# Zero-tile products in TensorE's early gaps and two moved weight steps, in a delta-rule attention kernel followed by two feed-forward layers

## The chip, the cores and the metric

The kernel runs on one core of a Trainium2 chip. The metric is the device time of one execution in microseconds (us), the median of several runs.

## What is computed

A delta-rule attention over 4 batches, 8 heads, 768 steps and head size 48; its output, 3072 tokens of 384 numbers, goes through a feed-forward layer of width 2048 and then through four experts of width 1024, mixed per token. All inputs are float32 but the first layer's two weight matrices, which arrive as float64.

```python
for t in range(S):                       # attention, per batch and head
    kt, vt, bt = (k_n[:, :, t], v[:, :, t], beta[:, :, t, None])
    y[:, :, t] = np.einsum('bhd,bhde->bhe', q[:, :, t], state)
    v_old = np.einsum('bhde,bhd->bhe', state, kt)
    state = state + bt[:, :, :, None] * np.einsum('bhd,bhe->bhde', kt, vt - v_old)
h = x @ w_in                             # first layer
x = (h * (1.0 / (1.0 + np.exp(-1.702 * h)))) @ w_out
for e in range(E):                       # four experts
    out += p[:, e:e + 1] * (np.maximum(x @ w1[e], 0.0) @ w2[e])
```

## The kernel before, in words

**Attention.** The 768 steps are cut into 12 units of 64 (u = 0 to 11), each worked for all 32 heads at once. Within a unit the steps depend on each other through a triangular matrix, which is inverted. Units come in pairs (w = 0, 2, 4, ...), and two units make a tile of 512 tokens. For the first pair `queue_first_inverse` runs the inverse on DVE: fourteen steps (L724, L726), `end` (L731), `to_rows` (L685, a transpose), `turn` (L750, another, once per unit). Then TensorE (PE) joins the halves of each matrix in `first` (L769) and `second` (L778), with a copy between them (`out1`, ACT) and a multiply-add behind them (`out2`, L783, DVE). `queue_q` multiplies keys with queries (L491, PE) and masks the products on DVE (L496, four times 0.7 us a unit).

`queue_chain` does the rest of a unit in two halves hu = 0 and 1: `solve` (L881, PE), copies of its result (`solved`, L184), `cross` (L896, PE), a subtraction (`rest`, L874, DVE), `solve` again and its copies, `fourth` (a copy into `stage`, L184), `read` (L912 and L913, PE), which makes the output rows, and `write` (L936, PE), which updates the state. For u = 0 and 1 the output rows go straight into the first layer's input: `take_x` (L184, `xs<-y`, three copies a half, a high part) and `take_rest` (L930, DVE, the low part). `direct[0]` is the list of these twelve tasks of unit 0.

**First layer.** Its width is cut into 16 blocks f = 0 to 15 of 128. A tile takes `layer1` (L1089, `ph`), the activation (`gate`: L1211, L1213, L1214) and `layer2_1` (L1196, `px`) for each block. Numbers are split in a high and a low part, and three products of the parts stand for one (`PASSES`). The first two tiles' first eight blocks go in halves of 256 tokens, so that unit 0 alone lets the layer begin. From there PE does the layer's products with the remaining attention woven in, and then the experts (L1323, L1353).

**Weights.** A block's weights come as float64 and are decoded on the chip in `queue_w1`: `load` (a DMA of 768 KB), `small` (ACT, L293) on the upper words and `low` (ACT, L296) on the lower ones, `shift` (DVE, L300) which joins them, `hi` (ACT, L305) and `lo` (DVE, L308), the two parts. `low` waits for the load and for the inverse's beginning, not for `small`. Blocks 0 and 15 land in the tile `raw`, the others in six buffers `rw`. Blocks 2 to 6 have a `touch` (L274, a DVE memset of one column) ahead of the load, which waits for one of five `marks`, in this order: the inverse's `begin`, its seventh step, the first `turn`, the last `first` of unit 0, the `out2` of unit 0. Block 7 and those after it wait for the `lo` of six blocks earlier.

**What sets the order.** Each engine runs its instructions in the order in which they were issued, and so does SP, which starts the DMAs. A planner (`Order`, `Task`) fixes that order when the program is made: each task has an engine or a choice of two, a cost, tasks that it waits for and a priority (small goes first). The planner keeps a clock per engine; whenever one is free it issues the task with the smallest priority among those ready at that time. Unit 0's chain has priority 0, `take_x` and `take_rest` have -2, the weights 6 (blocks 0 and 1), 16 (2 to 7) and 33. Until the first layer begins, PE tasks count double (`slow`).

Of the kernel before, what the change touches and what calls it, by code (L numbers as in the profile page):

```python
# [7 lines left out]
F32 = mybir.dt.float32  # L8
# [19 lines left out]
class Order:  # L28
# [14 lines left out]
    def task(self, fn, eng, cost, deps=(), lat=0.15, prio=0, slack=0.5, can=None, extra=0.4):  # L43
        t = Task(self, fn, eng, cost, [d for d in deps if d is not None], lat, prio, slack, can, extra)
        return t
# [106 lines left out]
def delta_attention_moe_moe_kernel(  # L152
# [12 lines left out]
    nc = tc.nc  # L165
# [92 lines left out]
    def queue_w1(f, after):  # L258
# [56 lines left out]
        if wide:  # L315
            a = task(small, "ACT", 0.83, (dep,), **kw)
            b = task(low, "ACT", 0.9, (dep, begun[0]), **kw)
            dep = task(shift, "DVE", 0.88, (a, b), **kw)
# [50 lines left out]

    NR, zeros = {}, {}  # L370
    spare = wp.tile([128, 1536], F32, name="sp", tag=f"w{RAW - 1}")
    jmask = spare[:, 0:SB * SB // 4].rearrange("p (a b) -> p a b", a=SB // 2)
# [96 lines left out]
    def queue_q(u):  # L469
# [11 lines left out]
        for o in range(2):  # L481
# [19 lines left out]
            if len(visits) == whole:  # L501
                t = task(lambda fs=tuple(visits): weave(fs), "PE", 0.9 if u < 2 else 1.3,
                         (*placed[u], lq, begun[0], *(ends[-1:] if u > 1 else ())), prio=p + 1,
                         can=lambda: None if u > 1 and not od.moe else some_free(banks(), whole))
                for c, f in masks:
                    c.setdefault("end", []).append(task(f, "DVE", 0.69, (t, zeros["pm"]), prio=p + 1))
                    ends.append(c["end"][-1])
                visits.clear()
                masks.clear()
# [177 lines left out]
    def queue_first_inverse(us):  # L687
# [65 lines left out]

        marks.append(turned[0])
        merged, products = [], []
        turns[w] = turned[0]
        for c, u in enumerate(us):
# [4 lines left out]
            def first(gn, c=c, ends=ends):  # L762

                if not gn.start:
                    cell["p", c] = bank([128, 2, NP, H], ends)
                t = cell["p", c]
                for g in range(NP)[gn]:
                    for r in range(0, 128, SB):
                        mm(t[r:r + SB, 0, g, :], lhsT=GG[w][r:r + SB, c * NP + g, :],  # L769
                           rhs=cell["d"][r:r + SB, c * NP + g, 0:H], start=True, stop=True, tile_position=(r, r))  # L770

            def out1(e, gs=gs, c=c):
                copy(e, cell["d"][:, gs, 0:H], cell["p", c][:, 0])

            def second(gn, c=c, u=u):
                for g in range(NP)[gn]:
                    for r in range(0, 128, SB):
                        mm(cell["p", c][r:r + SB, 1, g, :], lhsT=cell["d"][r:r + SB, c * NP + g, :],  # L778
                           rhs=Tb[u][r:r + SB, g, H:], start=True, stop=True, tile_position=(r, r))

            def out2(u=u, c=c):
# [29 lines left out]
    def queue_chain(u):  # L811
# [153 lines left out]
        for hs in [halves[0:1], halves[1:2]] if u < 2 else [halves]:  # L965
            n = len(hs)

            def both(name, *args, hs=hs):
                return lambda: weave([lambda h=h: h[name](*args) for h in hs])

# [20 lines left out]
            else:  # L991
                bs = [lv]
            a = task(both("solve", 0), "PE", 0.4 * n, (*bs, invdone[u]), prio=p, can=None if u else room)
            bs = solved_tasks(a, not u)
            a = task(both("cross"), "PE", 0.38 * n, (*bs, *crossed[u]), prio=p)
            bs = [task(h["rest"], "DVE", 0.47, (a,), prio=p) for h in hs]
            a = task(both("solve", 1), "PE", 0.4 * n, bs, prio=p)
            for h in hs:
# [95 lines left out]
    with tc.manual_schedule():  # L1094
# [32 lines left out]
        for n, fn, cost in (("j", set_j, 0.6), ("q0", lambda: E_.memset(PQ[0], 0.0), 1.85),  # L1127
                            ("su", lambda: E_.memset(SU, 0.0), 1.4), ("st", lambda: E_.memset(stage, 0.0), 1.4),
                            ("pm", set_p, 2.1), ("q1", lambda: E_.memset(PQ[1], 0.0), 1.85), ("h", set_h, 1.0),
                            ("g", set_g, 1.1)):  # L1130
            zeros[n] = task(fn, "POOL", cost, (), prio=2)
        od.clk["POOL"], od.clk["HW"] = 0.8, 1.1

# [333 lines left out]
```

## Time and profile before

| | |
|---|---|
| median of 3 runs | 1365.65 us (1365.31 to 1365.78) |
| profiled execution, its own time | 1365.22 us |
| its span, first to last instruction | 1363.3 us |
| PE busy | 1332.3 us, 98% |
| DVE, ACT, POOL busy | 612.2, 423.1, 221.3 us |
| DMA | 63.30 MB |

The profile has a row for each group of instructions: the line of the program that made it, the engine, the tiles written and read (`out<-in`, buffer numbers left out), how many, and the time. PE is the matrix product, PEld the loading of its weights, SPq the queue that issues DMAs. In a timeline each row is a run of equal instructions: start, length, what it is, and in brackets how long the engine had been idle before it and what ended that. A float32 product stands as two matmul records, a product of the split parts (fp32r) as one.

### The profile page before, as it was taken

The page shows a single profiled execution, that of the slowest core. Times are in us where ns is not written, and L with a number is a line of the kernel's source. Part 1 is how long each engine was busy: PE and PEld are TensorE (multiplying, and loading weights), DVE is VectorE, ACT ScalarE, POOL GpSimd, SP SyncE. Part 2 cuts the span into 40 slices and gives each one's busy share as a digit, 9 for nine tenths or more (in the row PEclk, how much of TensorE's full clock was granted, in tenths as well). Part 3 has the DMA queues.
Part 4 walks back from the last instruction along what each step waited for, and adds up shares of the span by engine and source line. Part 5 has one row for each costly group of instructions (what it writes and reads, how often), then busy time and mean ns, then how long its engine had stood idle before and what let it go on. Part 6 is the DMA issues. An engine that isn't in the chain of part 4 may idle for free.

```text
span 1363.3 us, 28151 instructions
## 1 busy us (share of the span) xinstructions
PE 1332.3 (98%) x12376; PEld 1118.1 (82%) x12376; DVE 612.2 (45%) x1049; ACT 423.1 (31%) x790; POOL 221.3 (16%) x408
## 2 busy tenths in 40 slices
PE   5899999999999999999999999999999999999998
PEld 4788898778787888788888888888888888888888
DVE  7888584663735224223333234433343333233443
ACT  6873442432424334312222122222222221112111
POOL 4295748055181000000000000000000000000000
PEclk9999999999999999999999999999999999999999
DMA  7640412220201013000010000010010000011111
GB/s 238 217 132 14 113 29 76 63 64 2 74 17 40 5 76 124 8 9 31 31 42 20 1 20 31 32 38 14 0 31 31 32 20 8 0 31 31 32 31 47
DMA packets 36411, 63.30 MB, mean 46 GB/s; under 512 B 18688, under 2 KB 20160, under 8 KB 36288
## 3 DMA queue, kind: packets, MB, share of 16 engines
q1 hardware_dynamic: 36288, 61.50, 14.9%
q8 instruction: 97, 1.59, 0.5%
q14 instruction: 26, 0.21, 0.1%
HBM read 52.58 MB, written 7.91 MB: 44 GB/s over the span
## 4 chain that ended last, share of the span: by engine, by line
PE 92%; DVE 4%; DMA 1%; ACT 1%; issue 1%; SPq 0%; DVEq 0%; ACTq 0%
PE ph L1089 43%; PE po L1323 24%; PE px L1196 14%; PE po L1353 5%; PE y L913 2%; PE ch L881 1%; PE ch L867 1%; PE gp L491 1%; PE ch L896 1%; PE ch L936 1%; DMA rw<-in_w_dram 1%; DVE scr L581 1%; PE gp L554 1%; DVE scr L685 0%; DVE scr L184 0%
## 5 line engine op out<-in xcount | busy, mean ns | idle before, releaser
L1089 PE MATMUL ph<-xs,w 128*128 128x512 f32 (+1 forms) x2736 | 651.3, 380 | 1.7 <-ACT x L184 0.8
L1089 PEld LDWEIGHTS ph<-xs,w 128*128 128x128 f32 x2736 | 494.2, 188 | 96.8 <-ACT x L184 1.2
L1384 DVE SCALAR_TENSOR_TENSOR hh<-ph,hh 128x512 fp32r<-128x512 f32 x192 | 132.5, 690 | 503.4 <-ACT hh L1383 503.4
L1323 PE MATMUL po<-hh,w 128*128 128x512 f32 x1440 | 352.4, 389 | 0.0
L1323 PEld LDWEIGHTS po<-hh,w 128*128 128x128 f32 x1440 | 270.4, 188 | 56.0
L1383 ACT ACTIVATE hh<-ph 128x512 fp32r<-128x512 f32 x192 | 114.8, 598 | 616.7 <-PE ph L1089 616.7
L1196 PE MATMUL px<-gh,w 128*128 128x512 f32 (+1 forms) x1008 | 228.7, 364 | 1.0 <-DVE gh L1214 0.8
L1196 PEld LDWEIGHTS px<-gh,w 128*128 128x128 f32 x1008 | 170.7, 188 | 31.6 <-DVE gh L1214 2.1
L1214 DVE TENSOR_TENSOR gh<-ph,gh 128x512 fp32r<-128x512 f32 (+1 forms) x112 | 68.7, 613 | 149.2 <-ACT gh L1213 148.0
L1211 ACT ACTIVATE ph<-ph 128x512 f32<-128x512 f32 (+1 forms) x112 | 58.4, 521 | 176.0 <-PE ph L1089 164.7
L660 POOL TENSOR_TENSOR scr<-scr,itmp 128x30 f32<-128x30 f32 (+9 forms) x150 | 83.9, 559 | 11.8
L658 POOL TENSOR_TENSOR itmp<-scr 128x30 f32<-128x30 f32 (+9 forms) x150 | 79.5, 530 | 11.2
L1353 PE MATMUL po<-w,hh 128*128 128x384 f32 x384 | 73.9, 342 | 0.0
L1353 PEld LDWEIGHTS po<-w,hh 128*128 128x128 f32 x384 | 69.3, 188 | 2.4
L1213 ACT CAST gh<-ph 128x512 fp32r<-128x512 f32 (+1 forms) x112 | 58.8, 525 | 3.5
L184 ACT COPY su<-ch 64x384 f32<-64x384 f32 (+2 forms) x59 | 27.2, 462 | 63.2 <-PE ch L881 62.5
L1183 DVE TENSOR_TENSOR xs<-x,xs 128x512 fp32r<-128x512 f32 x72 | 45.3, 684 | 0.0
L1182 ACT CAST xs<-x 128x512 fp32r<-128x512 f32 x72 | 39.7, 619 | 0.0
L496 DVE TENSOR_TENSOR pq<-gp,pmask 64x512 f32<-64x512 f32 x48 | 33.1, 689 | 7.0 <-PE gp L491 6.1
L250 DVE TENSOR_TENSOR w<-raw,w 128x768 fp32r<-128x768 f32 x32 | 30.7, 958 | 10.2 <-ACT w L249 9.4
L184 DVE COPY su<-ch 64x384 f32<-64x384 f32 (+2 forms) x45 | 24.2, 537 | 21.3 <-PE ch L881 20.4
L953 DVE TENSOR_TENSOR su<-su,ch 48x384 f32<-48x384 f32 x44 | 24.3, 552 | 20.5 <-PE ch L936 10.3
(133 smaller groups left out, 740.8 us busy)
## 6 DMA issues: line engine op xcount, KB each, us to landing
raw<-in_we_dram SPq DMA_DIRECT2D x32, 384.0 KB, 2.9
rw<-in_w_dram SPq DMA_DIRECT2D x14, 768.0 KB, 4.6
raw<-prd SPq DMA_DIRECT2D x20, 256.0 KB, 3.1
k<-in_k_dram SPq DMA_DIRECT2D x12, 384.0 KB, 4.8
kt<-in_kt_dram SPq DMA_DIRECT2D x24, 192.0 KB, 5.0
pq<-in_q_dram SPq DMA_DIRECT2D x24, 192.0 KB, 3.5
v<-in_v_dram SPq DMA_DIRECT2D x12, 384.0 KB, 3.2
out_dram<-oacc SPq DMA_DIRECT2D x80, 48.0 KB, 1.7
```

Source lines behind the costliest of these rows:

```text
L184: (nc.scalar.copy if e == "ACT" else nc.vector.tensor_copy)(out=out_, in_=in_)
L658: E.tensor_tensor(out=tv, in0=x[:, j:j + 1, j + 1:].broadcast_to([128, m, r]), in1=x[:, 0:m, j:j + 1].broadcast_to([128, m, r]), op=ALU.mult)
L660: E.tensor_tensor(out=x[:, 0:m, j + 1:], in0=x[:, 0:m, j + 1:], in1=tv, op=ALU.add)
L1089: mm(ps, lhsT=w[:, a, kk * 128:(kk + 1) * 128], rhs=xs[kk][:, b, cs], start=kk == 0 and i == 0, stop=kk == KD - 1 and i == 2)
L1196: mm(px[d][:, cs], lhsT=w[:, a, 384 + d * 128:384 + (d + 1) * 128], rhs=gh[:, b, 0:cs.stop - cs.start], start=f == 0 and i == 0 and cs.sta ...
L1211: a = task(lambda: nc.scalar.activation(out=ph, in_=ph, func=AF.Gelu_apprx_sigmoid), "ACT", 0.05 + 0.43 * c, (pe,), **kw)
L1213: a = task(lambda: nc.scalar.copy(out=hi, in_=ph), "ACT", 0.05 + 0.43 * c, (a,), **kw)
L1214: a = task(lambda: nc.vector.tensor_tensor(out=lo, in0=ph, in1=hi.bitcast(F32), op=ALU.subtract), "DVE", 0.07 + 0.53 * c, (a,), **kw)
L1323: mm(po[kk], lhsT=w[:, a, 384 + kk * 128:384 + (kk + 1) * 128], rhs=hh[:, c, :], start=f == 0 and i == 0, stop=f == F2 - 1 and i == 2)
L1353: mm(ps, lhsT=hh[:, a, b * 128:(b + 1) * 128], rhs=w[:, c, 384:768].rearrange("p (k a i) -> p a k i", a=4, k=KD), start=f == 0 and i == 0, ...
L1383: nc.scalar.activation(out=hh[:, 0, :], in_=ph, func=AF.Relu)
L1384: nc.vector.scalar_tensor_tensor(out=hh[:, 1, :], in0=ph, scalar=0.0, in1=hh[:, 0, :].bitcast(F32), op0=ALU.max, op1=ALU.subtract)
```

## The change

Three things are changed.

- A tile `still` of zeros (one of the two `gh` buffers, set by one DVE memset at the very start) and a PSUM tile `idle` (one of the two `ph` buffers). `fill(n)` multiplies the zeros with themselves n times, 128 x 128 by 512 columns, into `idle`, which nobody reads. The planner is not told of it. It stands behind unit 1's key-query products (8), behind unit 0's `first` and `second` (2 each), and in unit 0's second half behind `solve`, `cross` and `solve` (2 each): 18 products.
- `small` of blocks 7 and later waits, in the planner, for `direct[0]` too.
- The third mark is the inverse's `end` in place of the first `turn`: block 4's `touch` and load wait for that.

```diff
         if wide:
-            a = task(small, "ACT", 0.83, (dep,), **kw)
+            a = task(small, "ACT", 0.83, (dep, *(direct[0] if f >= 7 else ())), **kw)
             b = task(low, "ACT", 0.9, (dep, begun[0]), **kw)
             dep = task(shift, "DVE", 0.88, (a, b), **kw)
...
     NR, zeros = {}, {}
+    still = ghp.tile([128, 2, TT], F32R, name="gh", tag="gh")[:, 0]
+    idle = psh.tile([128, TT], F32, name="ph", tag="ph")
+
+    def fill(n):
+        for _ in range(n):
+            mm(idle, lhsT=still[:, 0:128], rhs=still, start=True, stop=True)
+
...
             if len(visits) == whole:
-                t = task(lambda fs=tuple(visits): weave(fs), "PE", 0.9 if u < 2 else 1.3,
+                def products(fs=tuple(visits)):
+                    weave(fs)
+                    if u == 1:
+                        fill(8)
+
+                t = task(products, "PE", 0.9 if u < 2 else 1.3,
...
-        marks.append(turned[0])
+        marks.append(ended[w])
         merged, products = [], []
...
+                if not c:
+                    fill(2)
 
             def out1(e, gs=gs, c=c):
...
+                if not c:
+                    fill(2)
 
             def out2(u=u, c=c):
...
-            def both(name, *args, hs=hs):
-                return lambda: weave([lambda h=h: h[name](*args) for h in hs])
+            def both(name, *args, hs=hs, more=0):
+                def products():
+                    weave([lambda h=h: h[name](*args) for h in hs])
+                    if not u:
+                        fill(more)
+
+                return products
...
-            a = task(both("solve", 0), "PE", 0.4 * n, (*bs, invdone[u]), prio=p, can=None if u else room)
+            a = task(both("solve", 0, more=2 if hs[0]["hu"] else 0), "PE", 0.4 * n, (*bs, invdone[u]), prio=p, can=None if u else room)
             bs = solved_tasks(a, not u)
-            a = task(both("cross"), "PE", 0.38 * n, (*bs, *crossed[u]), prio=p)
+            a = task(both("cross", more=2 if hs[0]["hu"] else 0), "PE", 0.38 * n, (*bs, *crossed[u]), prio=p)
             bs = [task(h["rest"], "DVE", 0.47, (a,), prio=p) for h in hs]
-            a = task(both("solve", 1), "PE", 0.4 * n, bs, prio=p)
+            a = task(both("solve", 1, more=2 if hs[0]["hu"] else 0), "PE", 0.4 * n, bs, prio=p)
...
+        nc.vector.memset(still.bitcast(F32), 0.0)
         od.clk["POOL"], od.clk["HW"] = 0.8, 1.1
```

## Rows read from the trace of the kernel before

**Rows 1.** The page, part 1: busy us, share of the span, instructions.

```profile
PE 1332.3 (98%) x12376; PEld 1118.1 (82%) x12376; DVE 612.2 (45%) x1049; ACT 423.1 (31%) x790; POOL 221.3 (16%) x408
```

**Rows 2.** Busy time by stretch: length; PE, PEld, DVE, ACT, POOL; granted clock, DMA.

```profile
53.30:1363.30 1310.00, 1301.92 (x11231) 1090.81 (x11231) 567.92 (x948) 386.42 (x719) 204.43 (x370) 1.00 0.13 39
```

**Rows 3.** Timeline of PE, 24 to 54 us: start, length, what, idle before.

```profile
24.91 2.27 PE L491 MATMUL gp<-pq,kt 48*64 48x64 f32 x61 [2.80 <-issue]
29.92 1.90 PE L769 MATMUL gp<-scr,scr 32*32 32x16 f32 x128 [2.74 <-DVE rw L274]
32.30 1.14 PE L778 MATMUL gp<-scr,scr 32*32 32x16 f32 x67 [0.48 <-ACT scr L184]
35.54 1.04 PE L778 MATMUL gp<-scr,scr 32*32 32x16 f32 x61 [2.10 <-issue]
37.30 1.50 PE L881 MATMUL ch<-v,scr 32*32 32x48 f32 x64 [0.72 <-issue]
39.59 1.75 PE L896 MATMUL ch<-su,g 32*32 32x48 f32 x64 [0.80 <-ACT su L184]
...
45.05 0.49 PE L912 MATMUL y<-pq,stage 128*64 128x64 f32 x4 [1.04 <-DVE stage L184]
...
50.37 1.64 PE L936 MATMUL ch<-su,k 64*48 64x48 f32 x64
52.62 0.38 PE L1089 MATMUL ph<-xs,w 128*128 128x256 f32 x1 [0.61 <-ACT xs L184]
53.30 0.86 PE L1089 MATMUL ph<-xs,w 128*128 128x256 f32 x5 [0.29 <-DVE xs L930]
```

**Rows 4.** Groups by line, 45 to 50.3 us, then 78.6 to 86 us.

```profile
L912 PE MATMUL y<-pq,stage 128*64 128x64 f32 x48 | 5.2, 317 | 1.0 <-DVE stage L184 1.0
...
L912 PE MATMUL y<-pq,stage 128*64 128x64 f32 x48 | 3.0, 227 | 0.3 <-DVE xs L930 0.3
```

**Rows 5.** Busy time, 45 to 50 us: the column behind POOL's is the granted clock.

```profile
45.00:50.00 5.00, 4.95 (x92) 4.95 (x94) 4.43 (x5) 4.43 (x10) 0.87 (x1) 1.00 0.83 282
```

**Rows 6.** The page, part 5: count | busy us, mean ns of one | idle.

```profile
L1089 PE MATMUL ph<-xs,w 128*128 128x512 f32 (+1 forms) x2736 | 651.3, 380 | 1.7 <-ACT x L184 0.8
```

**Rows 7.** Timeline of DVE, 24 to 100 us.

```profile
26.17 0.69 DVE L731 TENSOR_TENSOR scr<-scr,bt 128x512 f32<-128x512 f32 x1
...
32.66 2.79 DVE L496 TENSOR_TENSOR pq<-gp,pmask 64x512 f32<-64x512 f32 x4
36.71 0.48 DVE L783 SCALAR_TENSOR_TENSOR scr<-gp,hmask,scr 128x256 f32<-128x256 f32 x1 [1.25 <-PE gp L778]
...
46.16 0.96 DVE L308 TENSOR_TENSOR w<-rw,w 128x768 fp32r<-128x768 f32 x1 [0.30 <-ACT w L305]
...
52.97 0.67 DVE L930 TENSOR_TENSOR xs<-y,xs 128x128 fp32r<-128x128 f32 x3
```

**Rows 8.** The page, part 3: queue, kind: packets, MB, share of 16 engines.

```profile
q8 instruction: 97, 1.59, 0.5%
```

**Rows 9.** The DMA queues between 33.2 and 33.5 us.

```profile
q1 hardware_dynamic: 9, 0.04, 34.6%
q8 instruction: 1, 0.02, 19.4%
```

**Rows 10.** Timeline of SP's DMA issues, 0 to 60 us; rows merge several issues.

```profile
29.82 7.75 SPq L222 DMA_DIRECT2D rw<-in_w_dram  x3
...
47.15 6.26 SPq L222 DMA_DIRECT2D rw<-in_w_dram  x3
```

**Rows 11.** Timeline of ACT, 0 to 60 us.

```profile
34.32 0.89 ACT L293 ACTIVATE rw<-rw 128x768 f32<-128x768 f32 x1 [2.08 <-DMA rw<-in_w_dram]
...
37.07 0.94 ACT L293 ACTIVATE rw<-rw 128x768 f32<-128x768 f32 x1 [1.09 <-DMA rw<-in_w_dram]
38.27 1.27 ACT L184 COPY su<-ch 32x192 f32<-32x192 f32 x4 [0.25 <-PE ch L881]
...
51.49 0.93 ACT L293 ACTIVATE rw<-rw 128x768 f32<-128x768 f32 x1 [0.69 <-DMA rw<-in_w_dram]
52.30 0.61 ACT L184 CAST xs<-y 128x128 fp32r<-128x128 f32 x3
```

## The prediction

> **What bounds the kernel now.** I read the page's busy times first: PE is busy 98% of the span, no other engine half of it [rows 1]. The busy time by stretch then says where PE's idle time is: from 53.30 us to the end PE is idle for 1310.00 - 1301.92 = 8.1 us in all [rows 2]. Before 53.30, where the first layer's second product starts [rows 3], it waits most of the time. So the time is the moment at which PE's unbroken work begins, plus about 1310 us of products that this change leaves alone. A microsecond saved ahead of 53.30 is a microsecond off the total, provided that DVE, ACT and the weights are as much earlier as PE.
>
> PE's timeline shows what comes before [rows 3]: the halves of the inverse are joined (L769, L778), with a stop of 2.10 us in the middle that no semaphore explains; then unit 0's chain, the reads from 45.05, the writes from 50.37, and the first layer at 52.62, which waits for ACT's rows and then for DVE's.
>
> **The clock.** The granted clock reads 1.00 from the start, at 45 to 50 us too [rows 5], but the products disagree. The 48 records of L912, with as many of L913 between them, take 5.2 us for unit 0 and 3.0 us for unit 1 [rows 4]: PE is at the lower of its two levels (1.2 GHz) in the first case and at the upper (2.4 GHz) in the second. I go by the durations. That is the slack the 18 zero products can take: they would have PE at the upper level some 20 us earlier.
>
> **Zero products, the first eight.** They start when unit 1's products end, 24.91 + 2.27 = 27.18 [rows 3], ahead of `first`, which can start at 29.92. L1089 has 651.3 us for 2736 products, most of them 512 columns wide: 0.24 us at the upper level [rows 6], so 0.48 at the lower, an estimate. Eight end between 29.1 and 31.0. `first` starts up to 1.1 us late; I take 0.6 (the level rising on the way). Once it has risen, `first` is at most half of its 1.90 us shorter, 0.95 [rows 3]. The two roughly cancel: 0, bounds -0.9 and +1.1. The memset of the tile is one DVE instruction at the start, hidden behind DVE's wait for the first load; without that cover it would cost as much as another 128 x 512 DVE instruction, 0.69 us [rows 7].
>
> **The ten others** stand behind `first` and `second` and in the second half's steps, two at a time, 0.5 us at the upper level and 1.0 at the lower, where PE waits 0.48, 0.72 and 0.80 us anyway [rows 3]. Upper: 0. Lower: 0.2 to 0.5 each, five times at most, of which the ACT steps below hide most: 0 to 2.0. I take 0.
>
> **The earlier load of block 4.** `end` is over at 26.17 + 0.69 = 26.86 [rows 7]; the load is issued near 27 and no longer at 29.82 [rows 10], 2.9 us sooner. On SP it now goes ahead of a load of unit 2's keys, which nobody needs for 20 us. ACT's first step on it, 34.32 after 2.08 us of waiting [rows 11], moves ahead of `out1` in ACT's order, near 31.4: `out1` may be up to 1 us later, hidden by what follows. What I expect it to move is the stop of 2.10 us in `second`. The queue q8 carries 97 packets of 1.59 MB / 97 = 16.4 KB [rows 8], and PE has 12376 matmuls and as many weight loads [rows 1]: 24752 / 97 = 255 instructions a packet. It is PE's program, in blocks, and the packet of that moment goes between 33.2 and 33.5 us [rows 9], when block 4's packets are just through. With that load out of the way the stop shrinks; I take 0.8 us left, bounds 0 and 2.10. The next to be late is DVE: its eight masks end at 32.66 + 2.79 = 35.45, so `out2` gains 36.71 - 35.45 = 1.26 us at most [rows 7], 0 at least. I take 1.2.
>
> The Trainium skill, in "Runtime: NRT & Kernel Launch", section "Instruction fetch mechanics", says that the program is fetched in blocks of 16 KiB ahead of need, "mostly hidden". The packet size agrees; the 2.10 us do not. By that rule the stop is something else and this part gains nothing.
>
> **What becomes of the 1.2 us.** ACT's copies of the first `solve` (38.27) stand behind block 5's `small`, which waits for its load until 37.07 [rows 11]; that load is issued between DVE's two sets of masks, whose time does not change. So the copies start at about 37.9, 0.4 sooner. The 1.2 come back only in part: block 6's load follows `out2`, so ACT is through with that block about 0.9 us sooner. Against it stand three shifts in the planner's order, which I followed with its costs alone (an order, no time): the second half's `rest` goes ahead of block 0's `lo`, block 5's `shift` ahead of block 1's `lo`, and `fourth` moves from DVE to ACT, behind the copies of both halves. Reads begin between 44.0 and 45.4, where they began at 45.05 [rows 3]; I take 44.8.
>
> **The reads** gain 5.2 - 3.0 = 2.2 us if the upper level holds until then [rows 4], 0 if not. They end near 48 and not at 50.3.
>
> **The rows and block 7.** ACT, in order, has `small` of block 7 at 51.49, after 0.69 us of waiting for the load, and the second half's rows behind it at 52.30 [rows 11]. The change makes `small` wait for the rows; `low`, its twin, still waits for the load alone. By the planner's costs block 7's load is issued at 45.50 (2.0 and 1.5 us: `low` ready at 49.00), ACT is free at 49.12 and the rows are ready at 49.45: `low` takes the place that `small` leaves, of about the same length. So the rows still stand behind that load, which follows block 1's `lo` (46.16 + 0.96 = 47.12 [rows 7]; issued at 47.15 [rows 10]) and lands 51.49 - 47.15 = 4.34 us after its issue. With block 1's `lo` ending between 46.3 and 47.7, `low` begins at 50.6 to 52.0, the rows 0.81 later (52.30 - 51.49), and DVE's low parts, 0.67 behind the rows now (52.97 against 52.30 [rows 7, 11]), let PE go at 52.4 to 53.8, against 53.30. I take 52.6: 0.7 us gained. Block 4's `hi` now goes ahead of four state copies, which spares PE up to 0.4 us behind its first two blocks. Together **1.1 us**, and most of what the reads gain is lost to ACT's order.
>
> **Sum.** The profiled execution took 1365.22 us, its span and 1.9 around it; 1365.22 - 1.1 = 1364.1. The median of the runs is 0.43 above that execution: **1364.5 us**. A measurement of this kernel can tell about 0.2%, 2.7 us, from no change, so this is no change.
>
> **Rivals.**
>
> *The rows come free (1362.6).* If `low` of block 7 lands early or is planned behind the rows, the second half's rows follow the reads and block 3's `hi`: 50.0 to 51.2 and not 52.30, PE's unbroken work begins near 50.9, and with the 0.4 and a part of the small waits behind 53.30 that is about 2.9 us less: 1365.5 - 2.9 = 1362.6; with every wait shifting along, 1361. For it: the diff names these rows, and nothing else needs PE or DVE there. Against it: `low` keeps its two conditions. If so, no `L296` stands between the last `hi` and the second `xs<-y` copies.
>
> *The level does not rise, or falls back before the reads (1366.2).* The trace has no zero product, and the one rise that it shows came after reads that keep PE busy for 5 us without a gap [rows 3, 4]. Then the reads stay at 5.2 us, the eight products cost up to 1.1 us and the pairs up to 2.0, less up to 1.2 for block 4's load: at most +1.9, 1367.5. Most of the pairs lie beside ACT's steps; I take +0.6 on the median, 1366.2. The skill, in "TensorE: Matmul & The Clock Gate", Part 1, says that half rate is the default and that activity lifts it, and idling brings it back; the durations of [rows 4] agree with the first, no row here shows the last.
>
> *PE's program does not keep up (1368.7, slower).* The fills add 36 instructions ahead of the reads, so the block borders move: the next one falls from the pause behind the first `solve` (39.59, hidden) into that `solve`. At the upper level PE takes a block's 128 products in about 128 x 3.0 / 96 = 4.0 us, and the stop at 33.44 to 35.54 shows that a block may come later than PE wants it. Each new stop on the chain costs 2.1 to 2.8 us (2.10 and 2.80 [rows 3]). One is hidden by block 5's `small`; it decides from the second on, in the reads: two of 2.1 less the 1.1 of gain is +3.1, 1365.65 + 3.1 = 1368.7. Against it: ACT's waits for loads cover most places.
>
> **How the numbers follow.** The forecast has 0.50, the free rows 0.27, the level 0.14, the program 0.09. Of the free rows about two thirds lie below 1362.9 (0.2% less), of the forecast a twentieth (bounds of several terms at once): faster 0.20. Slower than 1368.4 are the program's case and a little of the level's: 0.10. The rest, 0.70, is within 0.2%. The range goes from 1361.8 (half way between the free rows' two values) to 1367.5 (the level's upper bound); it leaves out the program's case, the far end of the free rows and what I have not seen, 0.2 together.
>
> **What would show it.** Right: unit 0's L912 take 3.0 us and not 5.2; the idle time before the second part of L778 falls below 1 us; `out2` is near 35.5; ACT has L296 waiting for a load just ahead of the second half's `xs<-y`; L1089 begins near 52; behind it PE's idle time stays near 8 us. Wrong: rows right behind block 3's `hi`; reads that take 5.2 us; an idle time of 2 us "by issue" in L881 or L912; or more than 3 us of new idle time behind 53, where DVE could turn out not to follow.

## The result, and the profile after

The changed kernel takes 1373.05 us (median of 4 runs, 1372.53 to 1374.49), the kernel before 1365.48 us beside it (1364.90 to 1365.78): a ratio of 1.0053, with a 95% interval of 1.0037 to 1.0069. It is 7.6 us slower, and the forecast was 1364.5 with a range up to 1367.5. The profiled execution took 1374.49 us, its span 1372.6.

First the page's part 1 of the changed kernel, then the busy time of the stretch from the first layer's second product to the end (columns as in [rows 2]).

```profile
PE 1341.8 (98%) x12394; PEld 1122.7 (82%) x12394; DVE 612.2 (45%) x1046; ACT 424.5 (31%) x793; POOL 222.7 (16%) x412
```

```profile
54.78:1372.60 1317.82, 1305.98 (x11232) 1093.74 (x11231) 568.30 (x945) 389.17 (x725) 206.26 (x374) 1.00 0.13 39
```

PE has 18 products more and is busy 9.5 us longer [rows 1]. Its unbroken work begins at 54.78 in place of 53.30, 1.5 us late, and then takes 1317.82 us in place of 1310.00 [rows 2]. So 7.8 of the 9.3 us that this execution lost lie **behind** the point where the prediction's sum ended. Of these, 1317.82 - 1305.98 = 11.84 us are idle time (8.08 before), 3.8 more; PE is busy 4.1 us more with the same products.

PE's timeline of the changed kernel, 24 to 64 us (start, length, what, idle time before). L376 is the zero product, L781 `first`, L792 `second`, L928 the reads, L952 the writes, L1110 the first layer.

```profile
28.65 3.71 PE L376 MATMUL ph<-gh 128*128 128x512 f32 x8
32.29 1.26 PE L781 MATMUL gp<-scr,scr 32*32 32x16 f32 x128
33.48 0.73 PE L376 MATMUL ph<-gh 128*128 128x512 f32 x2
34.19 0.66 PE L792 MATMUL gp<-scr,scr 32*32 32x16 f32 x57
35.95 1.15 PE L792 MATMUL gp<-scr,scr 32*32 32x16 f32 x71 [1.10 <-issue]
37.04 1.22 PE L376 MATMUL ph<-gh 128*128 128x512 f32 x2
...
47.28 0.34 PE L928 MATMUL y<-pq,stage 128*64 128x64 f32 x4 [0.90 <-ACT stage L184]
...
50.22 1.64 PE L952 MATMUL ch<-su,k 64*48 64x48 f32 x64
54.55 4.12 PE L1110 MATMUL ph<-xs,w 128*128 128x256 f32 x18 [2.69 <-ACT rw L296]
```

The reads' group, 45 to 51 us (busy us, mean ns), and the busy time by stretch; the column behind POOL's is the granted clock.

```profile
L928 PE MATMUL y<-pq,stage 128*64 128x64 f32 x48 | 2.9, 225 | 0.9 <-ACT stage L184 0.9
```

```profile
35.00:40.00 5.00, 3.68 (x134) 2.80 (x136) 3.09 (x6) 1.76 (x4) 0.00 (x0) 0.56 0.53 195
40.00:45.00 5.00, 5.00 (x126) 3.46 (x130) 4.44 (x9) 3.84 (x6) 0.00 (x0) 0.50 0.25 98
45.00:50.00 5.00, 4.10 (x127) 3.54 (x118) 4.70 (x6) 3.51 (x8) 0.00 (x0) 0.92 0.73 239
...
55.00:60.00 5.00, 4.89 (x143) 4.41 (x144) 3.67 (x7) 4.58 (x11) 0.00 (x0) 0.66 0.92 288
...
185.00:190.00 5.00, 5.00 (x32) 5.00 (x31) 4.93 (x10) 1.35 (x4) 0.00 (x0) 0.66 0.01 3
```

The eight zero products run at half rate (a granted clock of 0.5, the lower of PE's two levels) to their end (3.71 us, 0.46 each); the clock's record begins at 32.15 with the full rate, falls to a half from 35.56 to 45.80, and is full again for the reads, which take 2.9 us and not 5.2 [rows 4]. That gain is there. Then PE waits 2.69 us ahead of the first layer, and a stretch of half rate (56.04 to 59.45) falls into it; another comes at 185.75 to 189.16. Each lasts 3.41 us, in which half the work is done: 1.7 us lost each time, 3.4 of the 4.1.

ACT, DVE and the waits of PE behind 54.7 us (us in total, times, longest) in the changed kernel. L305, L308, L293 and L296 are `hi`, `lo`, `small` and `low`; L946 is `take_rest`, L1236 the low part of an activation.

```profile
49.73 0.94 ACT L296 ACTIVATE raw<-raw 128x768 uint32<-128x768 uint32 x1 [1.41 <-DMA raw<-in_w_dram]
50.55 0.91 ACT L305 CAST w<-rw 128x768 fp32r<-128x768 f32 x1
51.33 0.62 ACT L184 CAST xs<-y 128x128 fp32r<-128x128 f32 x3
51.80 0.94 ACT L305 CAST w<-rw 128x768 fp32r<-128x768 f32 x1
53.53 0.92 ACT L296 ACTIVATE rw<-rw 128x768 uint32<-128x768 uint32 x1 [0.80 <-DMA rw<-in_w_dram]
54.82 0.43 ACT L184 CAST xs<-y 128x128 fp32r<-128x128 f32 x2 [0.37 <-DVE xs L946]
```

```profile
48.35 0.96 DVE L308 TENSOR_TENSOR w<-rw,w 128x768 fp32r<-128x768 f32 x1 [0.30 <-ACT w L305]
...
53.06 1.14 DVE L308 TENSOR_TENSOR w<-rw,w 128x768 fp32r<-128x768 f32 x1
54.13 0.28 DVE L184 CAST xs<-y 128x128 fp32r<-128x128 f32 x1
54.44 0.29 DVE L946 TENSOR_TENSOR xs<-y,xs 128x128 fp32r<-128x128 f32 x1
...
117.32 1.10 DVE L308 TENSOR_TENSOR w<-raw,w 128x768 fp32r<-128x768 f32 x1
```

```profile
PE ph L1110 <- ACT rw L296: 2.7, 1, 2.7
PE px L1218 <- DVE gh L1236: 2.2, 4, 1.0
PE ph L1110 <- DVE xs L946: 1.1, 1, 1.1
```

On ACT block 7's `low` stands where `small` stood, waits 0.80 us for its load, and has rows of the second half behind it, as forecast. But it is not what PE waits for. The planner gave the first of the second half's three row copies to DVE, where it stands behind block 3's `lo` (53.06) and starts at 54.13. PE's first product reads these rows and starts 0.14 us after the copy's end. The profile, which infers what ended a wait, names ACT's `low` because that ends at nearly the same time. In mark_dep (below), where ACT and DVE have the same order but for the zeros' memset, it names the copy:

```profile
52.87 3.40 PE L1089 MATMUL ph<-xs,w 128*128 128x256 f32 x17 [1.90 <-DVE xs L184]
```

New is what follows: the last `lo` of the first layer (block 15's) comes at 117.32, and PE waits for activations. The kernel before has that `lo` 9.6 us earlier:

```profile
107.68 0.94 DVE L308 TENSOR_TENSOR w<-raw,w 128x768 fp32r<-128x768 f32 x1
```

### The profile page after: what moved, and what is told of

It is laid out like the page before. It is cut to its first block, busy times and chain, and to the rows that moved or that the text cites. A ratio compares the mean times of both kernels' runs of the same rounds, so it can differ in the third digit from the quotient of the medians.

```text
span 1372.6 us, 28193 instructions
## 1 busy us (share of the span) xinstructions
PE 1341.8 (98%) x12394; PEld 1122.7 (82%) x12394; DVE 612.2 (45%) x1046; ACT 424.5 (31%) x793; POOL 222.7 (16%) x412
## 4 chain that ended last, share of the span: by engine, by line
PE 93%; DVE 3%; DMA 1%; issue 1%; ACT 1%; POOL 1%; SPq 0%; DVEq 0%; ACTq 0%; POOLq 0%
PE ph L1110 42%; PE po L1345 24%; PE px L1218 14%; PE po L1375 5%; PE y L929 2%; PE ch L897 1%; PE ch L883 1%; DVE scr L593 1%; PE gp L498 1%; PE ch L912 1%; PE ch L952 1%; DMA kt<-in_kt_dram 1%; PE gp L566 0%; ACT g L184 0%; DVE pq L503 0%
## 5 line engine op out<-in xcount | busy, mean ns | idle before, releaser
L1110 PE MATMUL ph<-xs,w 128*128 128x512 f32 (+1 forms) x2736 | 653.6, 381 | 5.2 <-ACT rw L296 2.7
L1110 PEld LDWEIGHTS ph<-xs,w 128*128 128x128 f32 x2736 | 496.4, 189 | 100.6 <-ACT rw L296 2.8
L1236 DVE TENSOR_TENSOR gh<-ph,gh 128x512 fp32r<-128x512 f32 (+1 forms) x112 | 68.7, 614 | 150.7 <-ACT gh L1235 149.6
L1233 ACT ACTIVATE ph<-ph 128x512 f32<-128x512 f32 (+1 forms) x112 | 58.4, 521 | 173.4 <-PE ph L1110 161.6
L670 POOL TENSOR_TENSOR itmp<-scr 128x30 f32<-128x30 f32 (+9 forms) x150 | 78.6, 524 | 11.2
L844 POOL TENSOR_TENSOR v<-v,nr 128x192 f32<-128x192 f32 x36 | 18.1, 535 | 98.9 <-DMA v<-in_v_dram 98.9
```

The costliest lines, as they stand in the source:

```text
L670: E.tensor_tensor(out=tv, in0=x[:, j:j + 1, j + 1:].broadcast_to([128, m, r]), in1=x[:, 0:m, j:j + 1].broadcast_to([128, m, r]), op=ALU.mult)
L1110: mm(ps, lhsT=w[:, a, kk * 128:(kk + 1) * 128], rhs=xs[kk][:, b, cs], start=kk == 0 and i == 0, stop=kk == KD - 1 and i == 2)
L1233: a = task(lambda: nc.scalar.activation(out=ph, in_=ph, func=AF.Gelu_apprx_sigmoid), "ACT", 0.05 + 0.43 * c, (pe,), **kw)
L1236: a = task(lambda: nc.vector.tensor_tensor(out=lo, in0=ph, in1=hi.bitcast(F32), op=ALU.subtract), "DVE", 0.07 + 0.53 * c, (a,), **kw)
```

## The experiments

Ratios are to the kernel before on the same chip, with 95% intervals. "Start of the k-th product" compares the products that write `ph` (the first layer's, then the experts') one by one, counted from 0, which shows where a kernel falls behind; worked out from the traces, in us against the kernel before:

```
product            0     1    18    45    72   144   216   280   500  last
before, at      52.6  53.3  58.4  68.0  85.2 109.4 155.5 178.9 300.2 1354.6
changed kernel  +1.9  +1.5  +2.9  +3.5  +3.6  +6.9  +8.1 +10.5  +9.4  +9.4
dep8            +0.1  -0.1  +0.7  +5.5 +10.7 +11.8 +10.2 +13.0  +8.6 +15.4
after_no15      +1.4  +1.6  +2.5  +3.0  +3.6  +3.6  +3.7  +3.7  +3.4  +3.4
hand15          +0.1  +0.1  +0.9  +0.9  +0.9  +0.9  +1.0  +1.0  +0.5  +0.5
pairs_hand7     -0.8  +0.5  +2.3  +2.6  +2.9  +2.9  +3.0  +3.0  +2.6  +2.6
rows_first      -0.7  -1.2  +2.9  +4.0  +4.1  +4.1  +4.1  +4.1  +3.7  +3.7
pairs_lean      -2.1  -2.6  -2.5  -0.0  +1.3  +1.3  +1.4  +1.4  +1.0  +0.9
```

### Which of the three parts costs the time

**fills_only**: all 18 zero products, nothing else of the change. **mark_only** and **dep_only**: the third mark alone (`marks.append(ended[w])`), and the planner's new wait of `small` alone. **mark_dep**: both, that is the change without its zero products.

> The 18 zero products alone, the planner's order as before. Clock theory (the products bring the upper level early, and the chip takes it back when the chain pauses, so that half-rate stretches fall into the first layer's unbroken work): slower than before by 2 to 5 us, with at least one stretch of granted clock 0.5 behind the start of L1089's work. Order theory (the planner's order, moved by the third mark and by the new wait of block 7, makes block 1's low part and with it block 7's load late): within 1 us of before, block 7's load still issued near 47 us.

> The third mark alone, no zero products. Order theory: block 1's low part is about 1 to 2 us later than before (47.1 us), block 7's load and the second half's rows with it, first layer from 54 to 55 us, total slower by 1 to 4 us. Clock theory: no stretch at half rate behind 55 us, total within 1 us of before or faster by up to 1 (the stop in the second joining product is shorter).

> The wait of the eighth and later blocks' first step alone. Both theories of the early stage: the other step on the lower words takes its place on ACT ahead of the rows, so the first layer starts within 0.7 us of before. Order theory: total between -1 and +3 us, what there is coming from idle time of PE between 80 and 200 us. Clock theory: within 1 us of before.

> The change without its zero products. Order theory: most of the 7.6 us stay, slower than before by 4 to 6 us, with the waits of PE for DVE between 85 and 185 us that the changed kernel has, and no half rate behind 55 us. Clock theory: within 1.5 us of before.

Measured: zero products 1368.30 (1.0018, 1.0010 to 1.0027); mark 1367.06 (1.0005, 0.9996 to 1.0013); wait 1370.67 (1.0038, 1.0025 to 1.0050); mark and wait 1372.90 (1.0044, 1.0031 to 1.0057). So the wait, which the prediction priced by block 7 alone, is the largest part, and mark and wait bring 6.8 of the 7.6 us. The clock theory holds for the first two runs and misses the other two; their 4.5 and 6.8 us are also more than the order theory gave (up to 3, up to 6). The mark did what was forecast for it: `out2` comes at 35.72 in place of 36.71 [rows 7], and the stop inside `second` is 0.22 us in place of 2.10, while `second` waits 1.00 us for `out1` ahead of it in place of 0.48 [rows 3]. In mark_only:

```profile
33.08 1.14 PE L778 MATMUL gp<-scr,scr 32*32 32x16 f32 x67 [1.00 <-ACT scr L184]
34.44 1.04 PE L778 MATMUL gp<-scr,scr 32*32 32x16 f32 x61 [0.22 <-issue]
```

In total it gained nothing. The kernel without zero products has, in its profiled execution, the stretches of half rate too (55.01 to 61.84, 184.72 to 188.13), so they don't come from these products. Nor are they its main loss: its other four executions show a mean granted clock of 0.999 to 1.000 and still took 1370.71 to 1373.22 us.

### Which block's wait

**dep7**: the wait for block 7 alone, as below; **dep8**: for blocks 8 to 15 alone (`f >= 8`).

```diff
-            a = task(small, "ACT", 0.83, (dep,), **kw)
+            a = task(small, "ACT", 0.83, (dep, *(direct[0] if f == 7 else ())), **kw)
```

> The new wait for the eighth block alone (f == 7), all else as before. If what costs in the new wait is that the eight blocks behind it (8 to 15, block 15 among them, which is loaded early) decode later and crowd DVE and ACT between 85 and 190 us, this kernel is within 1 us of before, and the rows still wait behind the other step of block 7. If the cost lies in the eighth block's place itself, it is slower by 3 to 5 us, as with the wait for all of them (4.5).

> The new wait for blocks 8 to 15 alone, not for the eighth block. By the crowding theory slower than before by 3 to 5 us, the last low part (before: 107.7 us) 5 us or more later; by the other theory within 1 us of before.

Measured: block 7 alone 1365.94 (0.9996, 0.9987 to 1.0004): nothing. Blocks 8 to 15 alone 1381.08 (1.0099, 1.0086 to 1.0112), 14.4 us more. Of these only **block 15** counts: with the wait for 8 to 14 the planner issues every instruction in the place it had before, with the wait for 15 alone every one in the place it has in dep8. Block 15 lands early, in the tile `raw`, and the kernel before decodes it ahead of unit 0's rows, while PE does the reads:

```profile
46.95 0.95 ACT L293 ACTIVATE raw<-raw 128x768 f32<-128x768 f32 x1 [0.57 <-DMA raw<-in_w_dram]
```

ACT's timeline and PE's waits behind 53 us in dep8:

```profile
47.40 0.96 ACT L296 ACTIVATE raw<-raw 128x768 uint32<-128x768 uint32 x1 [0.69 <-DMA raw<-in_w_dram]
...
73.98 0.90 ACT L293 ACTIVATE raw<-raw 128x768 f32<-128x768 f32 x1
```

```profile
PE gp L778 <- issue: 3.3, 1, 3.3
PE px L1196 <- DVE gh L1214: 2.9, 4, 1.2
PE ph L1089 <- ACT xs L184: 1.3, 1, 1.3
```

`small` of block 15 moves not by 5 us but by 27, and the attention's later steps are laid differently among the products. The table shows the loss between products 18 and 72, far from the step itself. Over 8 of these 10 us are one stop of PE of 3.26 us that no semaphore explains (the `issue` row, from 66.99) and, right behind it, half rate from 70.51 to 80.75, an estimated 5.1 us. That waits for 15 alone cost 14.4 and for 7 and 15 together 4.5 says that the size belongs to the order that comes out, not to the step.

### Is it the step's place, or the planner's answer to the wait?

**after_no15**: the changed kernel with the wait for block 7 alone. **hand15**: the kernel before, with block 15's `small` and `shift` put behind unit 0's rows when the program is written out, so that the planner doesn't know of it and every other instruction stays where it was.

```diff
         def small():
+            if f == 15 and len(put_x) < 6:
+                behind.append(small)
+                return
```

> The changed kernel, but of the steps `small` only block 7's waits for unit 0's rows; block 15's does not (for blocks 8 to 14 the wait changes no instruction's place). Theory 'block 15' (its wait makes the planner lay the rest of the attention differently, and that is most of the loss): +2 to +4 us against the kernel before, so 4 to 6 us less than the changed kernel's +7.6; last `lo` of the first layer near 108 us again, as before, and not 117; the half rate behind the first layer's beginning may stay. Rival 'any change of order, or the zero products': +6 or more, with the later decode or the late stretches of half rate still there.

> Kernel before with block 15's `small` put, outside the planner, right behind the sixth row copy of unit 0 on ACT, and its `shift` right behind the sixth subtraction on DVE; all other instructions keep their order on all engines. Theory 'planner' (the step itself is cheap wherever it stands; the loss comes from what the planner does with the wait): within 1 us of the kernel before. Rival 'lateness' (block 15's step behind the rows takes ACT and DVE from the first gates, or keeps the tile `raw` too long): +4 us or more, as with the wait for blocks 8 to 15 alone (+14.4) or 7 to 15 (+4.5).

Measured: the changed kernel without block 15's wait 1368.74 (1.0019, 1.0009 to 1.0029), 2.9 us over the kernel before in place of 7.6. The step put by hand 1366.79 (1.0004, 0.9996 to 1.0013): it stands at 52.90 there, where the changed kernel has it later:

```profile
67.51 0.91 ACT L293 ACTIVATE raw<-raw 128x768 f32<-128x768 f32 x1
```

In after_no15, from the first layer's second product on, and its last `lo`:

```profile
54.95:1366.60 1311.65, 1303.29 (x11231) 1092.06 (x11231) 568.92 (x948) 387.71 (x720) 204.47 (x370) 1.00 0.13 39
```

```profile
111.25 0.94 DVE L308 TENSOR_TENSOR w<-raw,w 128x768 fp32r<-128x768 f32 x1
```

1311.65 us and not 1317.82; the two kernels keep step up to product 72 and part there. So some 4.7 of the 7.6 us (7.57 less 2.85, by the medians) are **the order that the planner makes of block 15's wait**; the step right behind the rows costs at most 1.8. In these two profiles the difference is 6.17 us, 3.48 of it idle time and 2.69 longer busy time; 1.7 of the latter are the half rate at 185.75, which after_no15 doesn't have. The step alone as late as 67.51 is not tested. It is a weak rival: its `shift` ends at about 77, and block 15's `hi` comes at 115.77. Which of the moved instructions costs what was not taken apart.

### Why the faster reads gave nothing

**eight_only** and **pairs_only**: the eight products, or the ten in pairs. **hand7**: no zero products, block 7's `small` by hand behind the rows. **pairs_hand7**: both of the last.

> The first eight zero products only, without the pairs. The level rises near 31 to 33 us. If the pairs are what holds it, it falls again within 10 us and the reads run at the lower level: +0.5 to +3 us (the eight push the first joining product back by up to 2.4). If it holds without them, reads of 3 us and the same total as with all of them (+2.2), since what they gain is lost on ACT and in half-rate stretches behind 55 us.

> Zero products in pairs only, without the first eight; the order as before. If the eight are what raises the level early, this kernel stays at the lower one until the reads, the pairs cost about 1 us each at most where PE waits anyway: 0 to +2 us against before. If the pairs alone raise it, granted clock 1.0 comes before 45 us, and the reads take 3 us in place of 5.

> Kernel before with block 7's `small` put, outside the planner, right behind the sixth row copy of unit 0 on ACT; nothing else moves. Theory 'rows free' (the second half's rows only stood behind block 7's load): rows follow the reads' end and block 3's `hi`, near 50.8 in place of 52.30; PE's first layer goes on without its 0.61 and 0.29 us of idle time, at 52.0 and 52.7; 0.4 to 0.9 us less in all. Rival 'the writes hold PE anyway, and weights come next': no difference, within 0.4 us.

> The ten zero products in pairs (no eight, no mark, no planner wait), with block 7's `small` by hand behind the rows as in the run hand7; no other instruction moves. Theory 'gain kept by freeing the rows': reads 2.8 us, PE's first layer at 50.3 to 51.0 (52.62 before, 53.00 with the pairs alone), idle time ahead of it below 0.8 us and not 2.6; total -0.5 to -2.0 us against before, where the pairs alone cost +2.3: the rest is eaten by a stretch of half rate behind the first layer's beginning. Rival 'the half rate and the weights take it all': no gain, 0 to +2 us, although the first layer begins 2 us sooner.

Measured: eight 1366.77 (1.0007, 0.9996 to 1.0018), pairs 1367.84 (1.0017, 1.0006 to 1.0027), hand7 1365.73 (1.0000, 0.9991 to 1.0008), both 1368.23 (1.0015, 1.0006 to 1.0023). The eight raise the clock at 31.58 and lose it at 34.99, long before the reads, which stay at half rate; `first` starts 1.7 us late. The pairs have it up by 42.85, and reads of 2.9 us. In hand7 the rows do come free, at 50.29 in place of 52.30, and it is worth nothing that can be measured. With the pairs as well PE's timeline (L1116 is the first layer) and its busy time read:

```profile
48.97 1.65 PE L958 MATMUL ch<-su,k 64*48 64x48 f32 x64
51.78 0.39 PE L1116 MATMUL ph<-xs,w 128*128 128x256 f32 x1 [1.16 <-ACT xs L184]
53.83 3.00 PE L1116 MATMUL ph<-xs,w 128*128 128x256 f32 x17 [1.67 <-DVE xs L952]
```

```profile
50.00:55.00 5.00, 2.17 (x38) 1.85 (x33) 4.47 (x10) 4.51 (x13) 3.81 (x4) 1.00 0.93 309
55.00:60.00 5.00, 5.00 (x144) 4.74 (x143) 4.22 (x6) 4.07 (x9) 0.00 (x0) 0.51 0.82 304
```

The first product is 0.8 us early, the second 0.5 late: DVE has a shift and a `lo` ahead of the low parts. While PE has 2.17 of 5 us to do, ACT and DVE have 4.5, and half rate follows (55.10 to 61.93). So the theory of the freed rows fell, and its rival, that half rate and weights take it all, holds; it gave up to 2 us more, 2.3 were measured.

### Is it the pause, or the early rise?

All profiles with the pairs so far had a pause of PE ahead of the first layer, and a stretch of half rate behind it.

**rows_first**: no zero products; by hand, the weight steps of blocks 2 and later that are issued after unit 0's first read are held back and issued behind the sixth low part of its rows. **pairs_rows_first**: the same with the pairs.

```diff
+        def behind(fn):
+            def step():
+                if started and len(put_r) < 6 and (f > 1 if fn is not load else f - 6 in kept):
+                    held_back.append(fn)
```

> Kernel before without zero products; outside the planner, every weight step of blocks 2 and later that was issued between unit 0's first read and its sixth low part of the rows goes behind that sixth low part (ACT and DVE do the rows first); nothing else moves. Theory 'rows held by weight steps': second half's rows right at the reads' end near 50.3, PE goes from the writes (52.0) into the first layer without a pause, second product near 52.1 and not 53.30; 0.5 to 1.2 us less in all. Rival 'weights next': blocks 2 and 3 are ready 2 us later, PE waits for them behind its first two blocks, no gain or +1.

> The same with the ten zero products in pairs. Theory 'the pause ahead of the first layer brings the half rate': reads 2.8 us, no pause over 0.8 us between reads and first layer, second product of the first layer near 51, and no stretch of half rate behind it (with the pairs alone there was one of 3.4 us, with block 7's step moved one of 6.8, both behind pauses of 2.6 to 2.8 us): 1.5 to 2.5 us less than the kernel before. Rival 'the half rate follows the early rise whatever PE does': the stretch is there again, and the gain is -0.5 to +1.5. Rival 'weights next': no stretch, but PE waits for blocks 2 and 3, -0.5 to +0.5.

Measured: 1370.06 (1.0029, 1.0018 to 1.0040) and 1370.41 (1.0037, 1.0024 to 1.0050), both slower. PE's timeline and busy time in rows_first (L1106 first layer, L780 `first` of the next pair, L1213 the second product):

```profile
51.91 2.42 PE L1106 MATMUL ph<-xs,w 128*128 128x256 f32 x18
54.26 1.28 PE L780 MATMUL gp<-scr,scr 32*32 32x16 f32 x128
58.77 2.73 PE L1213 MATMUL px<-gh,w 128*128 128x256 f32 x9 [3.22 <-ACT gh L1230]
```

```profile
55.00:60.00 5.00, 1.71 (x65) 1.32 (x54) 4.42 (x8) 4.89 (x11) 0.00 (x0) 0.74 0.94 307
60.00:65.00 5.00, 5.00 (x29) 5.00 (x28) 3.97 (x11) 3.66 (x7) 0.00 (x0) 0.58 0.83 303
```

The first layer begins 0.7 us early, its second product 1.2, and PE then waits 3.22 us for the first activation: ACT does the held weight steps first. A kernel without zero products now has a stretch of half rate (57.42 to 64.24), behind a pause. The rival 'weights next' was right in kind and too small by 2.7 us. The question for pairs_rows_first is not decided by it: it made a pause of 2.95 us at the same place, and has a stretch from 58.91.

**lean** and **pairs_lean** take work away ahead of the first activation: block 7's three decoding steps behind the second activation, block 15's behind the sixth, `lo` of blocks 2 and 3 behind the rows; without and with the pairs.

```diff
+                n = {7: 2, F1 - 1: 6}.get(f, 0)
+                if fn is lo and f in (2, 3) and len(put_r) < 6:
+                    held_back.append(fn)
+                elif fn is not lo and len(gates) < n:
+                    later_on.append((n, fn))
```

> Kernel before without zero products; outside the planner, what ACT and DVE need not do before the first activation of the first layer goes behind it: block 7's `small`, `low` and `shift` behind the second activation, block 15's behind the sixth, the `lo` of blocks 2 and 3 behind unit 0's sixth low part. Nothing else moves. Theory 'ACT's and DVE's queues up to the first activation bound the start' (with the rows first alone, PE began 1.2 us sooner and then waited 3.2 us for the first activation, 57.94 in place of 55.85): first activation near 53, no pause over 0.8 us, no half rate; 0.8 to 1.3 us less. Rival 'weights next': a pause at a later block, same or slower.

> The same with the ten zero products in pairs. Theory as there: the reads' gain now reaches the first layer (second product near 51, first activation near 53, no pause, no stretch of half rate): 1.5 to 2.6 us less than the kernel before. Rival 'the half rate follows the early rise whatever PE does': no pause, and yet a stretch of half rate near 53 to 60; -0.5 to +1.5. Rival 'weights next': pause at a later block, 0 to +2.

Measured: 1374.05 (1.0063, 1.0051 to 1.0075) and 1370.44 (1.0043, 1.0029 to 1.0057), so both theories fell. In lean PE pauses 0.69 and 1.44 us near 62 us, and half rate lasts from 65.29 to 82.35, 8.5 us by the reckoning above. The profile of pairs_lean is of its fastest run, 1366.16 (the others took 1369.73 to 1375.72); L1125 is the first layer, L1233 the second product, L1252 an activation's low part:

```profile
50.52 2.42 PE L1125 MATMUL ph<-xs,w 128*128 128x256 f32 x18
...
61.27 1.22 PE L1233 MATMUL px<-gh,w 128*128 128x256 f32 x8 [1.53 <-DVE gh L1252]
```

```profile
50.00:55.00 5.00, 4.67 (x175) 4.25 (x171) 4.91 (x9) 4.41 (x10) 3.42 (x4) 1.00 0.66 256
55.00:60.00 5.00, 4.66 (x36) 4.26 (x35) 3.71 (x7) 4.28 (x7) 0.00 (x0) 1.00 0.91 321
60.00:65.00 5.00, 3.73 (x145) 3.40 (x146) 4.62 (x17) 2.95 (x5) 1.44 (x2) 1.00 0.86 236
```

Here the reads' gain reaches the first layer: it begins at 50.52, 2.1 us early, its second product 2.6 early, no pause above 0.4 us until 59.7, and the clock stays at full rate from 43.05 to the end. So in this execution the early rise alone brought no half rate. Of the five others, 3.6 to 9.6 us longer, three show a mean granted clock of 0.992 to 0.996, so they had it; two show 0.999 and 1.000 and were 3.8 and 4.7 us longer without it, for a reason that stays open. And still, in the profiled one, the lead is gone by product 45: PE is idle 1.27 us in 60 to 65 and waits for DVE, which does the next unit's chain ahead of an activation in an order made for a PE that comes later. That is the rival 'weights next' in a wider form. None of these versions measurably beats the kernel before.

## Why the prediction was wrong, and where it was right

**The step that failed** is the one in the first part, "plus about 1310 us of products that this change leaves alone". They took 1317.82 us. The diff's wait is for blocks 7 *and later*; the prediction followed it for block 7, step by step, and never asked where the other blocks' `small` stood. One of them, block 15's, stood ahead of the rows, and was thereby moved. In its place the runs show 4.7 us from the planner's new order, and 2.9 that stay with block 7's wait, the mark and the zero products together. Against the sum (1364.1, this execution 1374.49) that term is off by 7.8 us, the start by 2.2 (54.78 for 52.6), and the rest is the 0.4 for block 4's `hi`, which no figure shows. Its list of what would make it wrong had "more than 3 us of new idle time behind 53, where DVE could turn out not to follow"; 3.8 came, and the waits name DVE. But no rival carried it: the one on the slower side, PE's program, was another mechanism. Its stops moved (1.10 and 0.37 us in `second` and `solve`), none fell into the reads.

**The first eight** were put at 0 (-0.9 to +1.1). They took all the 3.71 us at half rate: the level rose as they ended, not on the way. `first` came 2.4 us later than before, 1.5 of them since unit 1's key-query products ended later in this execution; it is 0.64 us shorter (1.26 against 1.90 [rows 3]). Alone (eight_only) they have `first` 1.7 us late, 0.8 of them for that same reason. So their own delay is 0.8 to 0.9 us, inside the bound; with the shorter `first` it nearly cancels, as was taken, and the total was not measurably changed (1.0007).

**The ten others** at 0 (to 2.0): alone 1.0017 (2.3 us; 1.2 by the medians), and that in spite of the reads' gain.

**Block 4's load**: right. The stop inside `second` was 1.09 to 2.66 us in the eight profiles without the early load or zero products, 2.10 before; with the early load it was 0.22 (mark_only), none (mark_dep) and 1.10 (the changed kernel). `out2` came 1.0 us earlier in mark_only, where 1.2 was taken. By the Trainium skill's "Runtime: NRT & Kernel Launch", section "Instruction fetch mechanics", the fetch is mostly hidden and this part should have moved no stop. The traces don't agree for these early stages: stops of up to 4.0 us that no semaphore explains (1.10 and 1.70 in the changed kernel, 3.99 in fills_only) end shortly behind a packet of PE's program, as told at the end.

**The order**: right in each of its three shifts, and in that they eat the gain: block 7's load stands behind block 1's `lo`. That `lo` ended at 49.31 (from 48.35), and at 48.13 in mark_only; 46.3 to 47.7 was given, so its forecast was at least 0.4 us too early. In mark_only the reads begin at 46.15, 1.1 us later than before, although `out2` came 1.0 us earlier; 44.0 to 45.4 was given.

**The reads**: right, 2.9 us and not 5.2. That they would begin at 44.8 was not: 47.28, 46.35 in after_no15.

**The rows and block 7**: ACT's order is right (`low` in `small`'s place, 0.80 us of waiting, rows behind it), but it did not decide. PE was let go at 54.78, where 52.6 was taken, by DVE: by the row copy that the planner had moved there behind block 3's `lo`, and the low part after it. That the distance from block 1's `lo` to PE's second product came out near the old one, 54.78 - 48.35 = 6.4 us against 53.30 - 46.16 = 7.1 [rows 3, 7], is luck. What made this path late was not priced: ACT waits 1.41 us for block 15's load, 0.57 before, and lands it at 49.73 in place of 46.95; the `hi` steps that DVE's `lo` of blocks 2 and 3 need stand behind it. In after_no15 the rows do stand behind `low` on ACT, at 53.69.

**The rival of the free rows** was priced at 2.9 us and had 0.27. hand7 frees them and gains nothing measurable; its place in the sum was wrong, since ACT and DVE have their own work to do before the first activation, whatever PE does.

**What half rate does** was seen as a danger up to the reads only. The prediction took it that, once up, the level stays. It fell behind pauses of PE in the first layer, where the products are dense and each us counts in full. The Trainium skill, in "TensorE: Matmul & The Clock Gate", Part 1, does say that idling brings half rate back; the prediction cited that and left it without a price, "the last" that no row showed. The traces now show half rate behind pauses of PE, though not behind each.

Two readings of the prediction are off and carry nothing. Up to 53.30 PE waits 53.30 - (1332.3 - 1301.92) = 22.9 us, less than half of the time [rows 1, 2]. And the free rows' sum starts from 1365.5, where the median is 1365.65.

## What to carry to other kernels

A planner's wait that is added for a whole class of tasks has to be followed for each member: the one that had stood elsewhere may lay the rest of the program anew, and such an order can cost more than the step. Before an engine's early stage is shortened, read what the *other* engines have to do up to the point where it needs them next: at 4.5 of 5 us busy, ACT and DVE decide when the dense work goes on, and a lead of PE turns into a pause. A pause that is longer than before is paid twice when the clock falls behind it. And what a profile names as the end of a wait is inferred: ask which instruction wrote what the waiting one reads.

## What the runs showed of the hardware

- Products of zeros raise PE's clock too: after eight of 128 x 128 by 512 the record shows full rate from 31.58 (eight_only) or 32.15, where the kernel before came to it at 50.25.
- The early rise does not hold by itself: between small products (32 x 32 tiles, 48 columns) and two zero products at a time PE stayed at half rate from 35.56 to 45.80, though it was busy 5.00 of 5 us from 40 to 45. Among the same products it rose at 42.85 in pairs_only, without the eight ahead.
- Half rate came back soon after PE's first pauses behind the reads where these were 1.16 and 1.67 us (pairs_hand7), 1.31 (dep8), 1.90 (mark_dep), 2.41 (fills_only), 2.63 (pairs_only), 2.69 (the changed kernel), 2.95 (pairs_rows_first), 3.06 (after_no15) or 3.22 (rows_first), and not where the pauses there stayed below 0.8 us (the kernel before, hand7, hand15, mark_only, dep7, eight_only). Pauses of 2.13 us (dep_only) and 1.53 (pairs_lean) had no such consequence, so the length alone does not decide; near 183 us in the changed kernel two of 0.49 and 1.03 with one product between them were enough. What exactly decides stays open.
- PE's stops "by issue" follow its program's packets. All 54 such stops of 0.87 us or more in the 18 profiles end 1.22 to 1.64 us after the end of a packet of q8 (16.4 KB, about 255 instructions [rows 1, 8]), worked out from the packets' times in the traces. In the kernel before the packet goes from 33.34 to 34.27 and PE goes on at 35.54; in mark_only it goes from 31.82 to 33.06, PE goes on at 34.44, and only 0.22 us of that is a stop. The stop of 3.26 us in dep8 is one of them (packet 67.39 to 68.61, PE on at 70.25).
